# A transformer block on one core: fewer warm-up matmuls, two clamps on VectorE, a later wait in front of two transposes, and new queue orders

## The chip, the core and the metric

The kernel runs on one core of a Trainium2 chip. A core has five engines with a queue each: TensorE (PE) for matmuls and transposes, VectorE (DVE), ScalarE (ACT), GpSimd (POOL) and SyncE (SP), which issues most transfers. Every queue is worked off in order; a semaphore makes an instruction wait for one of another engine. Sixteen DMA engines move the data. The metric is the device time of one execution in microseconds, the median of several runs.

## The reference

One block of a transformer on 2048 tokens of width 448: normalization, linear attention with 16 heads of 28, a residual, normalization, a gated GELU layer of width 1792, a residual.

```python
phi = lambda t: jnp.where(t > 0, t + 1, jnp.exp(t)) + 1e-6
x  = A_x                                          # 1 x 2048 x 448
q, k, v = heads(_layernorm(x) @ A_wqkv)           # 16 heads of 28
pq, pk  = phi(q), phi(k)
kv  = einsum("bhsd,bhse->bhde", pk, v);  z = pk.sum(tokens)
o   = einsum("bhqd,bhde->bhqe", pq, kv) / (einsum("bhqd,bhd->bhq", pq, z) + 1e-6)
h   = x + o @ A_wo
n   = _layernorm(h)
out = h + (gelu(n @ B_w_gate) * (n @ B_w_up)) @ B_w_down
```

## The kernel before

The tokens are cut into 16 tiles of 128. Every piece of work on a tile is a named task on one engine. The kernel first builds all tasks with what they read and write, from which come the semaphores; the order of the tasks on each engine is written out by hand, name by name, in `ORDERS` (lines 14 to 62), one string each for PE, ACT, DVE, POOL and SP. A task cannot run before the one in front of it in its engine's string. A number in a name is a tile (for `q` tasks, a chunk of four tiles and a half; for `gu` tasks a running number).

The stages, and the names:

- **Start.** `warm1` and `warm0` (line 454) are matmuls of ones on PE that nobody reads; they keep PE busy until there is work. Their number is `WARM` (line 253), 38.
- **First normalization.** `bnst`, `bnag` on DVE gather mean and variance (lines 462, 463), `negm` on POOL negates the mean, `ln`, `rstd` on ACT make the reciprocal deviation, `norm` (line 486 on DVE for tiles 0 to 3, line 487 on POOL for the others) writes `xn`. Tiles 0 to 3 are transposed on PE (`tr`, line 495) and copied out on ACT (`ev`, line 523). For the others ACT copies 64 columns behind the tile (`dup`, line 525), and SP issues a DMA transpose (`xT`, line 526).
- **k and v.** `k` and `v` tasks of PE together compute both projections of a tile in two PSUM banks. A matmul uses 64 of 128 rows, so that two run side by side, one on the upper half (A), one on the lower (B); `k` has K on half A and V on half B, `v` the other way round. Where two tasks swap the halves of a bank, the second waits until the first is complete. `ek` (ACT) takes the exponential of K, `cl` (POOL, line 566) clamps it to 0 and 1, `ph` (DVE, line 568) makes pk of both, `evv` (ACT, line 570) copies V. `acc..a`, `acc..b` (PE) add pk and v into banks 6 and 7, with the halves swapped between a and b.
- **q.** `qa`, `qb` on PE, `eq` and `rq` (exponential, relu, lines 616, 617) on ACT, `cq` and `pq` on POOL and DVE.
- **Attention output.** `kz1`, `kz2` (DVE, lines 642, 643) make the masked kv, `nd` on PE multiplies it with pq, `rd`, `om` (DVE) divide. Tiles 0 and 1 are transposed on PE (`tro`), tiles 2 to 15 by a DMA transpose (`oT`, line 729). `wo` on PE applies the output matrix, `hr` (DVE, line 660) adds the residual.
- **Second normalization.** For tiles 0 and 1 `normh` and `wrap` on DVE write `hn` (`wrap`, line 695, copies its first 64 columns behind the tile), `trh` transposes seven blocks of it on PE (line 702; only the last block reads the wrapped columns), `evh` copies them out. The others go through POOL and a DMA transpose (`hT`, line 750).
- **The gated layer.** `gu` on PE, `ge` (Gelu, ACT, line 830), `hm` (product, DVE, line 832), `down` on PE, `out` (DVE, line 756), `dout` (SP). `tbl2` loads ACT's table for Gelu before the first `ge`.

SP's string also holds the loads: the tiles of x and the weights of q first, then `xT4` to `xT15`, then `dwo..` (4 loads) and `dwg0 dwu0 ... dwu6` (14 loads of 224 KB), then `oT2 oT3 dwd` (1568 KB) and the transposes of the gated stage. All are issued from SP in this order.

Tasks whose waits are given by position (`mw=True`) wait in front of the matmul that needs the buffer and not in front of the whole task; `emit` calls `W(n)` for that.

Of the kernel before, what the change touches and what calls it, by code (L numbers as in the profile page):

```python
# [7 lines left out]
ALU = mybir.AluOpType  # L8
# [4 lines left out]

ORDERS = (
# [47 lines left out]
)  # L62


# [145 lines left out]
def _c_mm(n, cnt=1):  # L210
    return cnt * (n / 2400.0 + 0.0025)
# [6 lines left out]
def _c_dve(n, rate=1.0):  # L218
    return 0.06 + n / 960.0 / rate
# [11 lines left out]
def bass_sequential_preLN__linear_attn_block__glu_gated_geglu__prompt_kernel(  # L231
    nc, A_x, A_wqkv, A_wo, B_x, B_w_gate, B_w_up, B_w_down, out, cfg=None
):
    cfg = dict(cfg or {})
    S, D, FF = 2048, 448, 1792
# [5 lines left out]
    EPS = 1e-6  # L241
# [4 lines left out]
    NQC = S // QCH  # L246
    N_PE_TR = 4
    STAT_GROUPS = [[0], [1], [2], [3]] + [[t, t + 1] for t in range(4, T, 2)]
    EV_DVE = cfg.get("ev_dve", ())
    N_DVE_NORM = cfg.get("n_dve_norm", 4)  # L250
    N_PE_A2 = 2
    B1_CHUNKS = [2, 2, 4, 4, 4]
    WARM = 38
    WARM2 = 8
    N_END = 4
    Q_LATE = cfg.get("q_late", 5)
# [2 lines left out]
    G = _Graph()  # L259
    es = ExitStack()  # L260
    with es:
# [14 lines left out]
        ident = sb("ident", [128, 128], BF16)  # L276
# [4 lines left out]
        mones = sb("mones", [GP, 4], F32)  # L281
        eps_t = sb("eps_t", [128, 1], F32)
        mhalf = sb("mhalf", [128, 2], F32)
# [5 lines left out]
        ln1 = sb("ln1", [128, T], F32)  # L289
# [3 lines left out]
        ln2 = sb("ln2", [128, T], F32)  # L293
        rs2 = sb("rs2", [128, T], F32)
        xn = sb("xn", [128, T, 512], BF16)
        e1 = sb("e1", [128, 3, D], BF16)
        tm1 = sb("tm1", [128, 3, D], BF16)
# [26 lines left out]
        b_ident, b_ones, b_mask2, b_mask3, b_mtmp, b_mones = (_Buf(n) for n in ("ident", "ones", "mask2", "mask3", "mtmp", "mones"))  # L324
# [5 lines left out]
        b_hn, b_hnd = bufs("hn", HN_R), bufs("hnd", HN_R)  # L330
        b_hnT = bufs("hnT", HR)
        b_e1, b_tm1, b_pk, b_v1 = bufs("e1", 3), bufs("tm1", 3), bufs("pk", 4), bufs("v1", 4)
# [10 lines left out]
        def bank(*b):  # L343
            return [b_ps[x] for x in b]
# [24 lines left out]
        def op(eng, fn, r, w, name, dur, key=None, after=()):  # L369
            if key is None:  # L370
                ik[0] += 0.01
                key = ik[0]
            return G.add(eng, fn, r=r, w=w, name=name, dur=dur, key=key, after=after)
# [129 lines left out]
        for ts in STAT_GROUPS:  # L503
# [6 lines left out]
            for t in ts:  # L510
                dve = t < N_DVE_NORM
# [12 lines left out]
                else:  # L524
                    op("act", lambda e, t=t: e.activation(xn[:, t, D:512], xn[:, t, 384:D], AF.Identity), [b_xn[t]], [b_xnd[t]], "dup%d" % t, 0.105, kln)
                    xt = G.add("sp", lambda e, tok=tok, t=t: e.dma_start_transpose(xnT[:, :, tok], xn[:, t, :]), r=[b_xn[t], b_xnd[t]], w=[b_xnT[t]],
                               name="xT%d" % t, kind="dmat", dur=1.25, key=t - 3.0, after=xts[-1:])
# [14 lines left out]
        def kv_tile(t):  # L542
            kk = 6.5 + 1.75 * t
# [4 lines left out]
            def kmm(s, o_, v, st_, sp_):  # L548
# [14 lines left out]
            i, ie = t % 4, t % 3  # L563
            psK3 = oK.rearrange("p (g e) -> p g e", g=NG)
            act_exp(lambda e: e.activation(e1[:, ie, :], oK, AF.Exp), bank(bk), [b_e1[ie]], "ek%d" % t, _c_act(D), kk)  # L565
            op("pool", lambda e: e.tensor_scalar(tm1[:, ie, :], e1[:, ie, :], 1.0 + EPS, 0.0, ALU.min, ALU.max),  # L566
               [b_e1[ie]], [b_tm1[ie]], "cl%d" % t, 0.53, kk)
            op("dve", lambda e: e.scalar_tensor_tensor(pk[:, i, :, 0:GW], psK3, EPS, tm1[:, ie, :].rearrange("p (g e) -> p g e", g=NG), ALU.max, ALU.add),  # L568
               bank(bk) + [b_tm1[ie]], [b_pk[i]], "ph%d" % t, _c_dve(D), kk)
            op("act", lambda e: e.activation(v1[:, i, :, 0:GW], oV.rearrange("p (g e) -> p g e", g=NG), AF.Identity),  # L570
# [92 lines left out]
        def a2_first(t):  # L663

            ka = -20.0 + 0.1 * t
            bnd, bh = FIRST_BK[t]
# [28 lines left out]
            op("dve", lambda e: e.tensor_copy(hn[:, sh, D:512], hn[:, sh, 0:64]), [b_hn[sh]], [b_hnd[sh]], "wrap%d" % t, 0.09, ka)  # L695
            tvh = psb[:, bh, 0:896].rearrange("p (k t) -> p k t", k=7)

            def ftrh(e):
                ins = None
                for k in (0, 1, 2, 4, 5, 6, 3):  # L700
                    ko = k * 128 if k < 4 else (k - 4) * 128 + 64
                    ins = e.transpose(tvh[:, k, :], hn[:, sh, ko:ko + 128], ident[:])
                return ins
            G.add("pe", ftrh, r=[b_hn[sh], b_hnd[sh], b_ident], w=bank(bh), name="trh%d" % t, dur=_c_mm(128, 7), key=ka)
            hv_ = hnT[:, :, (t % HR) * 128:(t % HR + 1) * 128]
            if t % 2 == 0:
                exp_tasks.append(op("act", lambda e: e.activation(hv_, tvh, AF.Identity), bank(bh), [b_hnT[t % HR]], "evh%d" % t, _c_act(896), ka))
# [205 lines left out]
```

## Time and profile before

| what | us |
|---|---|
| median of 3 runs | 196.21 (196.19 to 196.62) |
| the profiled execution | 196.7 |
| its span, first to last instruction | 194.9 |
| PE busy | 190.3 |
| DVE busy | 116.3 |
| ACT busy | 78.2 |
| POOL busy | 42.0 |

A row of the timeline reads: start and duration in us from the start of the span, engine, line, operation, output<-inputs, their shapes, number of instructions in a row; in brackets the idle time of the engine before it and what ended it. Neighbouring instructions of the same kind are merged, so that one row can hold several tasks. A `q` behind an engine's name marks its sequencer, which issues a transfer; a row `DMA to landing` tells how long the transfers of the row above took from issue to the end. PEld is the loading of weights into PE and overlaps PE. A busy PE is not PE at its peak: a matmul's row is some 0.2 us longer than the time after which the next one can start. A row of the windows has the stretch, its length, the granted clock, the share of the 16 DMA engines that is busy and the GB/s.

### The profile page before, as it was taken

Reading aid. Unit: us, or ns where it says so; the run is one execution under the profiler, and the core shown is the slowest. Engines: PE = TensorE matmul, PEld = TensorE weight load, DVE = VectorE, ACT = ScalarE, POOL = GpSimd, SP = SyncE. Lnnn points to the kernel's source line nnn. Section 1 sums busy time; section 2 is a strip of 40 time slices with the busy share of each in tenths; the row PEclk is TensorE's granted clock in tenths of the full one; section 3 lists DMA queues with packets and bytes.
Section 4 is the critical chain, followed back from the end, with each engine's and each line's share of the span. In section 5 each row is a group of like instructions: output and inputs, shape, how many; then the busy total and the mean of one; then the engine's idle time right before and its main releaser. Section 6 shows DMA issues by size and latency. Waiting matters only on the chain.

```text
span 194.9 us, 5336 instructions
## 1 busy us (share of the span) xinstructions
PE 190.3 (98%) x2192; PEld 137.9 (71%) x2192; DVE 116.3 (60%) x301; ACT 78.2 (40%) x205; POOL 42.0 (22%) x90
## 2 busy tenths in 40 slices
PE   7999999999999999999999999999999999999994
PEld 7556658754588977976675577877778779899554
DVE  2989735368998946843967745756735443431512
ACT  3689866669784212220442441233232442411100
POOL 3099974300050310500500500500500000000000
PEclk9999999999999999999999999999999999999999
DMA  6944558999836052152062250172040000010111
GB/s 191 377 116 97 81 110 185 247 248 205 260 103 110 15 101 50 50 105 62 10 129 46 46 106 2 30 117 51 5 94 28 23 0 0 3 47 3 47 47 47
DMA packets 37256, 17.53 MB, mean 90 GB/s; under 512 B 28272, under 2 KB 36336, under 8 KB 37232
## 3 DMA queue, kind: packets, MB, share of 16 engines
q1 hardware_dynamic: 36352, 16.45, 36.8%
q10 hardware_dynamic: 880, 0.75, 1.2%
q8 instruction: 17, 0.28, 0.6%
q14 instruction: 7, 0.06, 0.1%
HBM read 8.72 MB, written 1.84 MB: 54 GB/s over the span
## 4 chain that ended last, share of the span: by engine, by line
PE 96%; issue 1%; ACT 1%; DVE 1%; POOL 0%; DVEq 0%; ACTq 0%; POOLq 0%
PE ps L430 87%; PE ps L780 6%; PE ps L454 2%; DVE x_sb L660 1%; PE ps L495 1%; ACT xn L617 1%; PE ps L681 0%; ACT xnT L523 0%; PE ps L672 0%; DVE x_sb L756 0%; POOL ones_bf L395 0%; POOL eps_t L398 0%; ACT pqT L616 0%; DVEq L196 0%; ACTq L196 0%
## 5 line engine op out<-in xcount | busy, mean ns | idle before, releaser
L430 PE MATMUL ps<-hnT,wgu_sb 64*128 64x512 bf16 (+1 forms) x980 | 90.4, 333 | 0.0
L430 PEld LDWEIGHTS ps<-hnT,wgu_sb 64*128 64x128 bf16 x980 | 64.5, 94 | 18.6 <-DVE hh L832 1.7
L830 ACT ACTIVATE gl<-ps 128x256 bf16<-128x256 f32 x112 | 36.9, 381 | 89.3 <-PE ps L430 88.2
L832 DVE TENSOR_TENSOR hh<-ps,gl 128x256 bf16<-128x256 f32 x112 | 42.5, 415 | 35.7 <-ACT gl L830 31.5
L430 PE MATMUL ps<-wd_sb,hh 64*128 64x448 bf16 x336 | 34.4, 349 | 0.0
L430 PEld LDWEIGHTS ps<-wd_sb,hh 64*128 64x128 bf16 x336 | 25.6, 94 | 6.2 <-DVE x_sb L756 0.2
L430 PE MATMUL ps<-wkv_sb,xnT 64*128 64x448 bf16 x192 | 22.4, 350 | 0.4 <-ACT xnT L523 0.4
L462 DVE BATCH_NORM_STATS2 st<-x_sb 128x6 f32<-128x448 bf16 x32 | 18.7, 611 | 2.6 <-DMA x_sb<-in_A_x_dram 2.6
L756 DVE TENSOR_TENSOR x_sb<-ps,x_sb 128x448 bf16<-128x448 f32 (+1 forms) x17 | 9.9, 591 | 16.6 <-PE ps L430 9.8
L474 POOL TENSOR_SCALAR ln<-mv 128x2 f32<-128x2 f32 x7 | 1.6, 223 | 75.0 <-DVE mv L463 74.9
L568 DVE SCALAR_TENSOR_TENSOR pk<-ps,tm 128x448 bf16<-128x448 f32 x16 | 9.8, 620 | 9.6 <-POOL tm L566 7.1
L430 PE MATMUL ps<-xnT,wq_sb 64*128 64x512 bf16 x112 | 14.9, 377 | 0.2 <-ACT xn L617 0.2
L430 PEld LDWEIGHTS ps<-wkv_sb,xnT 64*128 64x128 bf16 x192 | 10.1, 94 | 6.3 <-issue 0.8
L430 PE MATMUL ps<-wo_sb,oT 64*128 64x448 bf16 x98 | 12.1, 350 | 0.1
L660 DVE TENSOR_TENSOR x_sb<-ps,x_sb 128x448 bf16<-128x448 f32 x16 | 9.4, 618 | 4.6 <-PE ps L430 4.4
L780 PE MATMUL ps<-wd_sb,hh 128*128 128x448 bf16 (+1 forms) x70 | 10.8, 315 | 0.0
L566 POOL TENSOR_SCALAR tm<-e 128x448 bf16<-128x448 bf16 x16 | 8.9, 559 | 6.4 <-ACT e L565 5.5
L487 POOL TENSOR_SCALAR hn<-x_sb,nm,rs 128x448 bf16<-128x448 bf16 x14 | 10.0, 720 | 0.8 <-POOL rs L476 0.2
L565 ACT ACTIVATE e<-ps 128x448 bf16<-128x448 f32 x16 | 8.5, 541 | 3.5 <-PE ps L430 2.2
L780 PEld LDWEIGHTS ps<-wd_sb,hh 128*128 128x128 bf16 x70 | 6.7, 98 | 4.3 <-issue 0.4
L655 DVE TENSOR_TENSOR o_sb<-ps,rd 128x448 bf16<-128x448 f32 x16 | 9.4, 612 | 0.1
L570 ACT ACTIVATE v<-ps 128x448 bf16<-128x448 f32 x16 | 8.4, 542 | 2.1 <-PE ps L430 2.1
(69 smaller groups left out, 140.4 us busy)
## 6 DMA issues: line engine op xcount, KB each, us to landing
out_dram<-x_sb SPq DMA_DIRECT2D x15, 112.0 KB, 1.7
wgu_sb<-in_B_w_gate_dram SPq DMA_DIRECT2D x7, 224.0 KB, 6.1
wgu_sb<-in_B_w_up_dram SPq DMA_DIRECT2D x7, 224.0 KB, 6.4
wd_sb<-in_B_w_down_dram SPq DMA_DIRECT2D x1, 1568.0 KB, 8.3
x_sb<-in_A_x_dram SPq DMA_DIRECT2D x2, 448.0 KB, 5.3
wkv_sb<-in_A_wqkv_dram ACTq DMA_DIRECT2D x2, 336.0 KB, 3.7
x_sb<-in_A_x_dram SPq DMA_DIRECT2D x3, 224.0 KB, 4.2
wo_sb<-in_A_wo_dram SPq DMA_DIRECT2D x2, 336.0 KB, 4.4
```

Source lines behind the costliest of these rows:

```text
L430: ins = e.matmul(o_, l_, r_, start=s_, stop=p_, **kw)
L462: op("dve", lambda e: e.bn_stats(st[:, t, :], src_ap), [b_src], [b_st[t]], "%sbnst%d" % ("" if mv is mv1 else "h", t), 0.53, key, after=after)
L487: return lambda e: e.tensor_scalar(dst, src[:, t, :], nm[:, t:t + 1], rs[:, t:t + 1], ALU.add, ALU.mult)
L565: act_exp(lambda e: e.activation(e1[:, ie, :], oK, AF.Exp), bank(bk), [b_e1[ie]], "ek%d" % t, _c_act(D), kk)
L566: op("pool", lambda e: e.tensor_scalar(tm1[:, ie, :], e1[:, ie, :], 1.0 + EPS, 0.0, ALU.min, ALU.max), [b_e1[ie]], [b_tm1[ie]], "cl%d" % t ...
L568: op("dve", lambda e: e.scalar_tensor_tensor(pk[:, i, :, 0:GW], psK3, EPS, tm1[:, ie, :].rearrange("p (g e) -> p g e", g=NG), ALU.max, ALU ...
L655: op("dve", lambda e: e.tensor_tensor(o_sb[:, so, oc:oc + D].rearrange("p (a e) -> p a e", e=28), nd3[:, :, 0:28], rd[:, i, :].unsqueeze(2 ...
L660: op("dve", lambda e: e.tensor_tensor(h_sb[:, u, :], ps[:, b, 0:D], x_sb[:, u, :], ALU.add), bank(b) + [b_x[u]], [b_h[u]], "hr%d" % u, 0.5 ...
L756: op("dve", lambda e: e.tensor_tensor(x_sb[:, t, c0:c1], ps[:, bk, c0:c1], h_sb[:, t, c0:c1], ALU.add), bank(bk) + [b_h[t]], [bo], "out%d% ...
L780: ins = e.matmul(ps[:, bk, c0:c1], hh[:, j, hsl(t)], wd_sb[:, j, c0:c1], start=(j == 0), stop=(j == NJ - 1))
L830: G.add("act", lambda e, gi=gi, cs_=cs_, psG=psG: e.activation(gl[:, gi, cs_], psG[:, cs_], AF.Gelu_apprx_tanh), r=bank(BK_G[i]), w=[b_glh ...
L832: op("dve", lambda e, dst=dst, srcU=srcU, srcL=srcL: e.tensor_tensor(dst, srcU, srcL, ALU.mult), bank(BK_U[i]) + [b_glh], [b_ar[j_][t % HR ...
```

## The change

Three edits in the code, and new strings for all five engines.

- `WARM` is 33 instead of 38.
- `cl14` and `cl15`, the clamps of exp(K), run on DVE instead of POOL.
- `trh0` and `trh1` wait for `normh` in front of their first block, and for `wrap` in front of the last one.

```diff
+    CL_DVE = cfg.get("cl_dve", (14, 15))
...
-    WARM = 38
+    WARM = 33
...
-            op("pool", lambda e: e.tensor_scalar(tm1[:, ie, :], e1[:, ie, :], 1.0 + EPS, 0.0, ALU.min, ALU.max),
-               [b_e1[ie]], [b_tm1[ie]], "cl%d" % t, 0.53, kk)
+            op("dve" if t in CL_DVE else "pool", lambda e: e.tensor_scalar(tm1[:, ie, :], e1[:, ie, :], 1.0 + EPS, 0.0, ALU.min, ALU.max),
+               [b_e1[ie]], [b_tm1[ie]], "cl%d" % t, _c_dve(D, 4.0) if t in CL_DVE else 0.53, kk)
...
-            def ftrh(e):
+            def ftrh(e, W):
                 ins = None
-                for k in (0, 1, 2, 4, 5, 6, 3):
+                for n, k in enumerate((0, 1, 2, 4, 5, 6, 3)):
+                    if n in (0, 6):
+                        W(n)
...
-            G.add("pe", ftrh, r=[b_hn[sh], b_hnd[sh], b_ident], w=bank(bh), name="trh%d" % t, dur=_c_mm(128, 7), key=ka)
+            G.add("pe", ftrh, r=[b_hn[sh], (b_hnd[sh], 6), b_ident], w=bank(bh), name="trh%d" % t, dur=_c_mm(128, 7), key=ka, mw=True, pdt=_c_mm(128))
```

The strings differ in many places. Those that matter below, before and after, engine by engine:

```
PE   v5 k6 qa01 v6 qb01 k7 acc3a acc4a v7
     v5 acc3a k6 qa01 v6 qb01 acc4a k7
PE   k11 k12 v11 v12 k13 acc8b acc9b v13 k14 acc9a k15 acc10a v14
     k11 acc8b k12 acc9b v11 v12 k13 acc9a acc10a v13 k14 k15 v14
PE   acc12a acc12b acc13b qa20 acc13a acc14a qb20 acc14b acc15b acc15a qa11
     acc12a acc12b acc13b acc13a acc14a qa20 acc14b acc15b qb20 acc15a qa11
PE   qa31 wo2a qb31 wo2b trh1 trh0 nd4a nd4b gu1
     qa31 wo2a wo2b trh1 trh0 qb31 nd4a nd4b gu1
ACT  ek7 evv7 evv8 dup14 ek8 dup15 evv9 ek9 ek10 evv10
     ek7 evv7 dup12 ek8 evv8 ek9 dup14 evv9 dup15 ek10 evv10
ACT  hln0 hrstd0 eq14 evh0 tbl2 ge1_0 ge1_1 rq14
     hln0 hrstd0 evh0 eq14 tbl2 ge1_0 ge1_1 ge0_1 ge0_0 ge3_1 ge3_0 rq14
DVE  bnst6 ph0 bnst7
     bnst6 bnst7 ph0
DVE  ph13 ph14 ph15 kz1 kz2
     ph13 cl14 ph14 cl15 ph15 kz2 kz1
POOL negm8 cl2 cl3 norm8 norm9 cq1 cq0 negm10 negm12 cl4 norm10 norm11 cl5 norm13 norm12 cl6
     negm8 cl2 norm9 cl3 norm8 negm12 cq1 cq0 negm10 cl4 norm13 cl5 norm10 negm14 norm11 cl6
POOL cl6 negm14 cq3 cq2 cl7 norm14
     cl6 opad2 cq3 cq2 cl7 norm12 norm14
```

On SP the order up to `dwu6 oT2 oT3 dwd` is the same; later some neighbours of the same kind change places (`oT4 oT5`, `dout0 dout1` and the like). In the gated stage `gu` tasks stand closer together before a `down` task (`gu49 gu48 gu51 gu50 down8a` where `gu49 gu48 down8a gu50 gu51` stood), and pairs of `ge` and `hm` tasks change places.

More of the change, by code (lines that the diff above doesn't have):

```diff
@@ L15 @@
     "warm1 warm0 tr0 tr1 k0 v0 k1 tr2 tr3 v1 k2 acc0a k3 v2 v3 qa00 acc0b acc1b qb00 k4 acc1a acc2a v4 k5 acc2b acc3b"
[4 rows of a table removed]
[4 rows of a table added]
     " wo6b down0b nd8a gu11 nd8b gu10 gu13 gu12 down2a wo8a down2b wo8b gu15 nd10a gu14 nd10b gu17 gu16 gu19 gu18 gu21"
     " wo10a wo10b gu20 nd12a gu23 nd12b gu22 gu25 gu24 gu27 gu26 wo12a down4a wo12b gu29 nd14a gu28 nd14b gu31 down4b"
[36 rows of a table removed]
[31 rows of a table added]
+    "ones eps mhalf mones powwarm ident mask_a opad mask_b mask_c negm4 cl0 norm4 norm5 negm6 cl1 norm6 norm7 negm8"
[4 rows of a table added]
     "dx0 dx1 dx2 dwv_t dx4 dx6 dx8 dx12 dwq dwq_t dwq_u pqones xT4 xT5 xT6 xT7 xT8 xT9 xT10 xT11 xT12 xT13 xT14 xT15"
[3 rows of a table removed]
[3 rows of a table added]
 )
```

83 rows, old and new, of the table ORDERS are left out of this document.

## The prediction

> **What bounds the kernel now.** I read the page first, then the chain of waits, then the timeline around each place that the change touches.
>
> ```profile
> span 194.9 us, 5336 instructions
> PE 190.3 (98%) x2192; PEld 137.9 (71%) x2192; DVE 116.3 (60%) x301; ACT 78.2 (40%) x205; POOL 42.0 (22%) x90
> PE 96%; issue 1%; ACT 1%; DVE 1%; POOL 0%; DVEq 0%; ACTq 0%; POOLq 0%
> ...
> 2.00 4.17 PE ps L454 x38
> 37.55 0.05 issue
> 40.26 0.05 issue
> 52.26 1.17 DVE x_sb L660 x2
> 62.84 40.46 PE ps L430 x552
> 103.35 78.37 PE ps L430 x776
> ```
>
> The chain is TensorE nearly throughout. From 62.84 to 181.72 us two pieces of matmuls follow each other with 0.05 us between them: nothing can be won there without removing matmuls, and the change removes none. What can move lies before 63 us: the start, and the places where TensorE waits. So the question is how much earlier TensorE starts, and whether what it needs later also comes earlier. The profiled execution took 196.7 us: 194.9 us of span and 1.8 us around it. It is 0.49 us above the median of the runs, 196.21 us.
>
> **The change, part by part.**
>
> *Fewer warm-up matmuls.* The start, in order of time:
>
> ```profile
> 5.21 0.37 DVE L486 TENSOR_SCALAR xn<-x_sb,mv,rs 128x448 bf16<-128x448 bf16 x1
> 5.97 0.40 DVE L486 TENSOR_SCALAR xn<-x_sb,mv,rs 128x448 bf16<-128x448 bf16 x1
> 6.10 0.96 PE L495 MATMUL ps<-ident,xn 64*128 64x64 bf16 x20
> 6.68 1.08 ACT L523 ACTIVATE xnT<-ps 128x512 bf16<-128x512 bf16 x2 [0.83 <-PE ps L495]
> 7.43 0.74 PE L430 MATMUL ps<-wkv_sb,xnT 64*128 64x448 bf16 x6 [0.36 <-ACT xnT L523]
> 9.76 0.75 PE L495 MATMUL ps<-ident,xn 64*128 64x64 bf16 x20
> ```
>
> The 38 warm-ups of line 454 take 4.17 us, 0.11 each; five fewer free TensorE 0.55 us earlier, at 5.55. But tr0 needs norm0, which ends at 5.58. With a hand-over of 0.06 us (an estimate; DVE's last residual add, below, ends at 53.42 and its matmul starts at 53.47) tr0 starts at 5.64 instead of 6.10. Its copy ev0 and then k0 follow at their present distances, so k0 starts at 6.97: **-0.46 us**. The rest of the 0.55 is lost to norm0. tr1 needs norm1 (ends 6.37) and moves by only 0.14, but k1 is not due for another 1.5 us.
>
> The 20 transposes of tr0 and tr1 take 0.96 us, the same 20 of tr2 and tr3 0.75: the clock doubled in between. [...]
>
> *The reordered POOL queue gives a little back.* The order of norm8, norm9 and the clamps changes:
>
> ```profile
> 16.75 1.19 POOL L626 TENSOR_SCALAR tm<-e 112x512 bf16<-112x512 bf16 x2
> 17.39 1.29 DVE L627 SCALAR_TENSOR_TENSOR pqT<-ps,tm 112x512 bf16<-112x512 f32 x2
> 18.74 0.30 PEld L430 LDWEIGHTS ps<-wkv_sb,xnT 64*128 64x128 bf16 x6 [0.29 <-DVE pqT L627]
> ```
>
> Today k6 waits for pq0 (ends 18.68), which waits for the q clamps cq1, cq0 on POOL. POOL is full here and moves earlier with its first input. In the new order negm12 comes ahead of cq1, one operation of 0.2 us, so pq0 moves by only 0.25. But acc3a (0.10) is put before k6 and fills part of it. **+0.11 us**, bounds 0 and 0.25. TensorE is then 0.35 earlier.
>
> *The clamps of tiles 14 and 15 on VectorE.*
>
> ```profile
> 37.96 0.62 DVE L568 SCALAR_TENSOR_TENSOR pk<-ps,tm 128x448 bf16<-128x448 f32 x1 [1.71 <-POOL tm L566]
> L749 DVE COPY hn<-hn x14: 264/268/333, 58.6 to 141.1; 128x448 bf16<-128x448 bf16 x14
> ```
>
> The trace has no such clamp on DVE. Nearest rows: a copy of 128x448 (0.27 us) below, the normalization of 128x448 (0.37) above; I take 0.27, since a clamp has constants as the copy has none and norm0 reads two scalars per row. It hides in the 1.71 us in which DVE waits for POOL; if that cover were gone it would cost 0.27 to 0.37 each. ph14 and ph15 come some 0.4 and 0.8 us earlier, and acc13a, acc14a move ahead of qa20. That moves the bank swaps, it doesn't remove them: before, two sit back to back (the issue pieces at 37.55 and 40.26); after, acc12a-acc12b and acc13b-acc13a do. **0**, bounds -0.12 and +0.12.
>
> *The transposes of xn wait for ACT.* This is the part the diff hides. ACT runs its queue in order, and the new order is "ek9 dup14 evv9 dup15" where it was "dup14 ek8 dup15 evv9 ek9".
>
> ```profile
> 25.59 0.25 ACT L525 ACTIVATE xn<-xn 128x64 bf16<-128x64 bf16 x1
> 26.25 0.26 ACT L525 ACTIVATE xn<-xn 128x64 bf16<-128x64 bf16 x1
> 27.23 0.55 ACT L570 ACTIVATE v<-ps 128x448 bf16<-128x448 f32 x1 [0.72 <-PE ps L430]
> 27.67 0.98 ACT L565 ACTIVATE e<-ps 128x448 bf16<-128x448 f32 x2
> ...
> L526 SPq DMA_TRANSPOSE xnT<-xn x2: 1216/1216/1217, 26.1 to 27.4; - x2
> 28.64 3.19 SPq L364 DMA_DIRECT2D wo_sb<-in_A_wo_dram  x4
> 45.48 2.51 SPq L729 DMA_TRANSPOSE oT<-o_sb  x2
> ```
>
> dup14 and dup15 (the rows of line 525) stand before the wait for v9 now, which ends at 27.23. Afterwards dup14 stands behind ek9, which needs v9: ek9 starts at 27.23 - 0.35 = 26.88, dup14 0.44 later (the distance of evv9 and ek9) and ends at 27.57. So xT14 is issued at 27.6 instead of 26.1, xT15 1.3 later, and dwo, the first of 18 weight loads behind them on SP, at about 30.2 instead of 28.64: **1.6 us later** (a second path, norm12 put behind cl7 on POOL, gives 1.8; if dup14 moved as TensorE does, 1.2). The weights themselves have cover: the last lands at 48.4 (below), gu1 starts at 54.13. But these loads fill the DMA engines, and behind them come oT2 and oT3:
>
> ```profile
> 44.00:46.00 2.00, 1.00 1.02 242
> L364 SPq DMA_DIRECT2D wgu_sb<-in_B_w_up_dram x1: 597/597/597, 40.9 to 40.9; - x1
> DMA to landing us min/median/max: 7.5/7.5/7.5
> ...
> DMA to landing us min/median/max: 2.6/3.1/3.5
> oT<-o_sb SPq DMA_TRANSPOSE x14, 2.5
> pqT<-ones_bf SPq DMA_DIRECT2D x1, 16.0 KB, 5.3
> ```
>
> The DMA share at 44 to 46 us is 1.02 (242 GB/s): the stream is bound by bandwidth, so it ends as much later as it starts later. Its last load lands at 40.9 + 7.5 = 48.4; oT2, which at its median would land at 48.0, lands at 45.48 + 3.5 = 49.0, and oT3 at 46.7 + 2.6 = 49.3. A load of 16 KB took 5.3 us behind the first weights. So what is issued behind a full queue lands behind it. Shifted by 1.6, oT2 lands at 50.6 and oT3 at 50.9.
>
> [...]
>
> ```profile
> 50.07 0.94 PE L430 MATMUL ps<-wo_sb,oT 64*128 64x448 bf16 x8
> 50.83 0.83 PE L430 MATMUL ps<-xnT,wq_sb 64*128 64x512 bf16 x6
> 53.04 0.22 PE L430 MATMUL ps<-kvz,pqT 64*128 64x116 bf16 x1
> 53.47 0.82 PE L430 MATMUL ps<-kvz,pqT 49*128 49x116 bf16 x15 [0.21 <-DVE x_sb L660]
> 54.13 0.60 PE L430 MATMUL ps<-hnT,wgu_sb 64*128 64x256 bf16 x8
> ...
> 61.77 1.81 PE L430 MATMUL ps<-wo_sb,oT 64*128 64x448 bf16 x14
> 63.42 0.82 PE L430 MATMUL ps<-hnT,wgu_sb 64*128 64x256 bf16 x12
> ```
>
> wo2a is due at 50.07 - 0.35 = 49.72 and can start at about 50.65 (0.93 lost). Its second matmul needs oT3, at 50.95, which adds about 0.2. **+1.15 us**; bounds 0.6 (1.2 later) and 1.5 (1.8 later). Behind wo2a TensorE's queue holds everything; nothing fills the hole.
>
> *After it.* wo2a and wo2b now stand back to back, as wo4a and wo4b do: those take 61.77 to 63.42, 1.65 us, where wo2a takes 50.83 - 50.07 = 0.76 for eight matmuls and six need 0.57. The swap of halves costs 0.32 there. In return qb31 stands before nd4a and covers the two residual adds that it waits for, 53.04 to 53.47, 0.43. **-0.10 us**, bounds -0.4 and +0.3. trh's split wait buys nothing: its copies are done while wo2a waits. eq14 now stands directly before the table load, so the first Gelu can come some 0.2 us late, of which a started pair of matmuls takes up most; **+0.05**, bounds 0 and 0.2. The other reorderings (gu, hm, out) lie under the unbroken matmuls after 62.84: 0, bounds -0.1 and +0.2.
>
> Sum: -0.46 + 0.11 + 0 + 1.15 - 0.10 + 0.05 = +0.75: 197.45 us by the profiled execution. The median lies 0.49 below it. If that is a shorter start, the new kernel doesn't gain it, since its start is set by norm0; if it is the profiling, it carries over whole (196.96). I take the middle, **197.2 us**; own range 196.8 to 197.7.
>
> **The rivals.**
>
> *A, the transposes are not held up (not slower).* The stream starts late but ends early enough, or oT2 and oT3 pass it. It decides at wo2a: its slack now is 50.07 - 49.3 = 0.8 us, so up to 0.4 us of lateness costs nothing after a gain of 0.35. For it: the weights' issues run 7.5 us ahead of their landings. Against it: a share of 1.02. Price: -0.46 + 0.11 - 0.10 + 0.05 = -0.40; 196.3 us by the profiled execution, 195.8 by the median.
>
> [...]
>
> *C, the front isn't shortened* because the median execution already starts early: 196.21 + 0.05 + 1.15 - 0.10 + 0.05 = 197.4, inside the forecast's range.
>
> **How the numbers follow.** Forecast with C: 0.62; A: 0.28; B: 0.10. The range from 195.8 (A) to 197.8 leaves out B and A's tail. A measurement of this kernel tells 0.3%, 0.59 us, from no change, so faster means below 195.62, slower above 196.80. A with its terms at their good ends falls below in half its cases: faster 0.14. The other half of A and 0.05 of the forecast's low end are the same: 0.19. Slower: 0.67.
>
> **What would show it.** tr0 at 5.6 and k0 at 7.0 show the first term; dwo issued after 30 us on SP and oT3 landing near 51 show the stream; an idle TensorE of about 1 us before wo2a's matmuls, ended by DMA, shows the loss; no wait for DVE before nd4a shows the small gain. I am wrong if dwo is issued before 29.2, or if oT3 lands before 50; k0's matmuls at the slow pace would show B.

## The result and the profile after

The changed kernel takes 197.58 us in the median of 8 runs (197.07 to 200.83), the kernel before 196.31 (196.17 to 196.74) in 8 runs on the same chip: a ratio of 1.0055, interval 1.0041 to 1.007. The change costs about one microsecond. The run of 200.83 us, at a clock of 0.991, is left out of the ratio. The profiled execution of the changed kernel is its fastest, 197.07 us; that of before, 196.7 us, was one of its slower ones. So the two profiles differ by 0.4 us of span where the medians differ by 1.27 (1.04 between the medians once that run is left out).

The page of the changed kernel, first the span, then the shares of the chain of waits:

```profile
span 195.3 us, 5326 instructions
...
PE 90%; DVE 4%; ACT 2%; DMA 2%; issue 1%; SPq 0%; DVEq 0%
```

PE's share of the chain is 90% where it was 96%. Some 12 us more of the chain (6% of the span) lie outside TensorE, and where they do is the first thing to read. Some 4.5 of them lie ahead of k0, where the chain now runs through the first normalization and not through the warm-ups, and cost nothing. TensorE's timeline at the places that the prediction named:

```profile
5.65 0.41 PE L496 MATMUL ps<-ident,xn 64*128 64x64 bf16 x10 [0.46 <-DVE xn L487]
6.86 0.74 PE L431 MATMUL ps<-wkv_sb,xnT 64*128 64x448 bf16 x6
...
18.38 0.74 PE L431 MATMUL ps<-wkv_sb,xnT 64*128 64x448 bf16 x6
...
48.48 1.04 PE L431 MATMUL ps<-xnT,wq_sb 64*128 64x512 bf16 x8 [0.19 <-ACT xn L618]
49.65 2.19 PE L431 MATMUL ps<-wo_sb,oT 64*128 64x448 bf16 x14
...
53.32 0.81 PE L431 MATMUL ps<-kvz,pqT 64*128 64x116 bf16 x16
53.97 8.29 PE L431 MATMUL ps<-hnT,wgu_sb 64*128 64x256 bf16 x140
...
63.65 0.60 PE L431 MATMUL ps<-hnT,wgu_sb 64*128 64x256 bf16 x8
```

These rows are tr0, k0, k6, qa31, wo2a with wo2b, nd4a with nd4b, gu1 and gu4. One row of before has not been shown yet, qa31:

```profile
49.21 1.04 PE L430 MATMUL ps<-xnT,wq_sb 64*128 64x512 bf16 x8 [0.19 <-ACT xn L617]
```

Cut at these tasks, the two spans add up as follows (each number is the difference of two start times above and in the prediction):

| stretch | before | after | difference | predicted |
|---|---|---|---|---|
| start to k0 | 7.43 | 6.86 | -0.57 | -0.46 |
| k0 to k6 | 11.31 | 11.52 | +0.21 | +0.11 |
| k6 to qa31 | 30.47 | 30.10 | -0.37 | 0 |
| qa31 to gu1 | 4.92 | 5.49 | +0.57 | +1.15 and -0.10 |
| gu1 to gu4 | 9.29 | 9.68 | +0.39 | +0.05 |
| gu4 to the end | 131.48 | 131.65 | +0.17 | 0 |
| sum | 194.9 | 195.3 | +0.40 | +0.75 |

The first row flatters the change, because the two executions differ in the clock. The trace records the step of TensorE's clock from half to full at 6.86 us in the execution of before and at 4.57 us in this one, and the warm-ups start 0.107 us apart ahead of it and 0.056 behind it.

The loss lies in two places that follow each other, the wait before wo2a and the first matmuls of the gated layer. For the first, SP's timeline (xT12 to xT15, dwo and its three companions, oT2 and oT3) and the landing times of the last two:

```profile
25.30 6.09 SPq L527 DMA_TRANSPOSE xnT<-xn  x4
31.44 2.39 SPq L365 DMA_DIRECT2D wo_sb<-in_A_wo_dram  x4
...
44.75 2.51 SPq L732 DMA_TRANSPOSE oT<-o_sb  x2
...
DMA to landing us min/median/max: 4.0/4.4/4.8
```

dwo is issued at 31.44, 2.8 us later than before (28.64). oT2 lands at 44.75 + 4.8 = 49.55, and wo2a starts at 49.65; oT3 lands at 46.0 + 4.0 = 50.0, and the rest of wo2a starts at 50.13, as the chain below shows. Before, oT3 had landed at 49.4 and nothing waited. The predicted landing was 50.9: the stream started later than foreseen, but in this execution it also ran faster. The windows (stretch, length, busy time of PE, PEld, DVE, ACT and POOL, granted clock, DMA share, GB/s):

```profile
44.00:46.00 2.00, 2.00 (x22) 0.83 (x18) 1.97 (x6) 1.83 (x4) 0.00 (x0) 1.00 1.04 298
```

It moved 298 GB/s where the execution of before moved 242 in the same window, at the same full share. For the second place, the chain of waits (start, length, what):

```profile
49.87 0.19 DVE mv L464
...
50.13 0.93 PE ps L431 x7
...
52.77 0.92 ACT hnT L710
53.68 0.91 ACT pqT L617
54.62 1.28 ACT L853
55.91 0.39 ACT gl L833
56.40 0.75 DVE hh L835 x2
57.15 0.53 DVE pqT L619 x2
...
57.74 0.74 DVE hh L835 x2
...
58.70 0.74 DVE pqT L620
...
59.84 0.68 DVE hh L835 x2
60.56 2.47 PE ps L431 x35
```

From 52.77 to 60.56 TensorE doesn't set the end: ScalarE does (evh0, eq14, the table load tbl2, ge1), then VectorE (hm1, cq14 and cq10, hm0, wrap3, pq10, wrap2, hm3), and gu5 starts when hm3 frees its bank. Before, the chain was matmuls from 53.47 us on. VectorE's timeline of before at hm0, pq12 and hm3:

```profile
57.88 0.75 DVE L832 TENSOR_TENSOR hh<-ps,gl 128x256 bf16<-128x256 f32 x2 [0.24 <-ACT gl L830]
...
58.92 0.68 DVE L619 TENSOR_TENSOR pqT<-xn,pqT 112x1024 bf16<-112x1024 bf16 x1
59.52 0.75 DVE L832 TENSOR_TENSOR hh<-ps,gl 128x256 bf16<-128x256 f32 x2
```

Measured from the start of gu1, hm0 starts at 3.75 us before and at 3.77 after, so cq14 and cq10, which stand ahead of it now, cost nothing. hm3 starts at 5.39 before and at 5.79 after (59.76 on VectorE), the whole 0.4: between the two stands pq10, which takes 1.04 us (58.62 to 59.66), where pq12 with 0.68 stood.

The first line of the chain wants care: it names VectorE ahead of wo2a, but wo2a reads only oT and wo_sb. The releaser shown is the last of several by time; the landing of oT3 at 50.0 is what wo2a needed.

### The profile page after: what moved, and what is told of

It reads as the page before. It is cut to its first block, busy times and chain, and to the rows that moved or that the text cites. A ratio compares the mean times of both kernels' runs of the same rounds, so it can differ in the third digit from the quotient of the medians.

```text
span 195.3 us, 5326 instructions
## 1 busy us (share of the span) xinstructions
PE 189.9 (97%) x2187; PEld 126.9 (65%) x2187; DVE 117.2 (60%) x303; ACT 77.9 (40%) x205; POOL 41.9 (21%) x88
## 4 chain that ended last, share of the span: by engine, by line
PE 90%; DVE 4%; ACT 2%; DMA 2%; issue 1%; SPq 0%; DVEq 0%
PE ps L431 82%; PE ps L783 6%; DMA x_sb<-in_A_x_dram 2%; DVE hh L835 1%; DVE st L463 1%; ACT L853 1%; DVE x_sb L661 1%; PE ps L496 1%; ACT hnT L710 0%; ACT pqT L617 0%; PE ps L705 0%; DVE pqT L620 0%; PE ps L689 0%; PE ps L682 0%; PE ps L673 0%
## 5 line engine op out<-in xcount | busy, mean ns | idle before, releaser
L431 PE MATMUL ps<-hnT,wgu_sb 64*128 64x512 bf16 (+1 forms) x980 | 91.8, 333 | 0.1
L431 PEld LDWEIGHTS ps<-hnT,wgu_sb 64*128 64x128 bf16 x980 | 61.2, 94 | 23.9 <-DVE hh L835 5.2
L431 PE MATMUL ps<-wd_sb,hh 64*128 64x448 bf16 x336 | 35.3, 349 | 0.0
L431 PEld LDWEIGHTS ps<-wd_sb,hh 64*128 64x128 bf16 x336 | 21.1, 94 | 10.9 <-DVE x_sb L759 0.2
L431 PE MATMUL ps<-wo_sb,oT 64*128 64x448 bf16 x98 | 13.0, 350 | 0.4
L482 POOL TENSOR_SCALAR nm<-mv 128x2 f32<-128x2 f32 x13 | 3.0, 227 | 39.5 <-DVE mv L464 39.1
L488 POOL TENSOR_SCALAR hn<-x_sb,nm,rs 128x448 bf16<-128x448 bf16 x14 | 10.7, 768 | 0.8 <-POOL rs L477 0.2
L431 PEld LDWEIGHTS ps<-wo_sb,oT 64*128 64x128 bf16 x98 | 6.3, 94 | 4.5 <-PE ps L431 1.5
```

Source lines behind the costliest of these rows:

```text
L431: ins = e.matmul(o_, l_, r_, start=s_, stop=p_, **kw)
L482: op("pool", lambda e: e.tensor_scalar(nm[:, a:b], mv[:, a:b, 0], -1.0, None, ALU.mult), b_mv[a:b], b_nm[a:b], "%snegm%d" % ("" if mv is m ...
L488: return lambda e: e.tensor_scalar(dst, src[:, t, :], nm[:, t:t + 1], rs[:, t:t + 1], ALU.add, ALU.mult)
```

## The experiments

The kernel before was run beside each group: 196.5 us median in 32 runs beside the first four experiments, 196.66 in 25 beside the next four, 196.4 in 23 beside e9 to e11, 196.32 in 9 beside e12. Ratios are to before's runs of the same group; medians of different groups compare less well, since before's own differ by 0.35. Orders are given as the part of the string that differs.

### e1 and e2: the copies for the transposes early again, in the changed kernel

```diff
 ACT
-ek8 evv8 ek9 dup14 evv9 dup15 ek10 evv10
+ek8 evv8 dup14 ek9 dup15 evv9 ek10 evv10
```

> The changed kernel with two names moved in ACT's order: dup14 ahead of ek9, dup15 ahead of evv9. Theory (late weight stream): xT15 is issued near 29.1 us instead of 30.2 and dwo near 30.4 instead of 31.4; about 1.0 us less of wo2a's wait for oT2 and oT3 remains, so 0.5 to 1.0 us faster than the changed kernel, near 196.8 us. Rival (the loss is in the new order behind wo2a: back-to-back halves, and VectorE and GpSimd in the first gated tiles): no change from 197.6 us.

Measured: 198.02 us median (196.85 to 200.13, 9 runs), ratio 1.0067, interval 1.0036 to 1.0099. A miss, and a useful one. SP's and TensorE's timelines of e1, with the landing times of oT2 and oT3:

```profile
31.04 2.40 SPq L365 DMA_DIRECT2D wo_sb<-in_A_wo_dram  x4
...
DMA to landing us min/median/max: 5.0/5.4/5.8
...
50.58 0.35 PE L431 MATMUL ps<-wo_sb,oT 64*128 64x448 bf16 x1 [1.09 <-DVE hn L487]
51.09 1.72 PE L431 MATMUL ps<-wo_sb,oT 64*128 64x448 bf16 x13 [0.16 <-DVE hn L487]
```

dwo came only 0.4 us earlier, and not even this is the copies': xT12 to xT14 are issued at the same times as in the changed kernel, to 0.01 us, and only the issues of xT14 and xT15 took less, 3.0 us together instead of 3.4. Something ahead of dup14 held the queue: xT12, whose copy dup12 now waits for norm12 behind cl7. And in this execution the transposes took 5.0 to 5.8 us to land instead of 4.0 to 4.8: oT3 landed at 46.0 + 5.0 = 51.0, and wo2a's two parts started at 50.58 and 51.09 where the changed kernel's started at 49.65 and 50.13. So the loss at this place is some 0.9 us larger here, though dwo was issued earlier: the stream moved 251 GB/s from 44 to 46 us and not 298. e2 adds the other half:

```diff
 POOL, on top of e1
-cl4 norm13 cl5 ... cq2 cl7 norm12
+cl4 norm12 cl5 ... cq2 cl7 norm13
 ACT
-dup13 dup10 ln14 ... evv7 dup12 ek8
+dup12 dup10 ln14 ... evv7 dup13 ek8
```

> As e1, and norm12 and norm13 (POOL), dup12 and dup13 (ACT) change places, so that the transposes are ready in the order in which SP issues them. Theory: dwo near 29.2 us, no wait for a transfer at wo2a, 196.1 to 196.5 us, the whole loss undone. Rival: 197.4 to 197.6 us.

Measured: 196.8 us median (196.42 to 198.71, 12 runs), ratio 1.0028, interval 1.0007 to 1.0049. dwo is issued at 30.08 instead of 31.44 (29.2 was expected), and the median is 0.8 us lower. It lies between its theory and its rival, 0.3 us above before: oT2 landed at 49.78, and wo2a, which was due at 49.3, started at 49.87. There are two paths to a late dwo, one through dup14 and dup15, one through norm12 and dup12; undoing the first alone gains little while the second holds. 1.4 us of the delay stay: xT13, whose copy now stands where xT12's stood, is issued 0.6 us later than before, and the issue of xT15 takes 2.14 us instead of 1.22.

### e3: the late copies alone, in the kernel before

```diff
 ACT
-evv8 dup14 ek8 dup15 evv9 ek9 ek10 evv10
+evv8 ek8 evv9 ek9 dup14 dup15 ek10 evv10
```

> The kernel before with dup14 and dup15 moved behind ek9 in ACT's order, nothing else. Theory: dwo near 30.6 us instead of 28.6, oT3 lands near 51, wo2a waits about 1 us for transfers: 197.0 to 197.5 us. Rival: the kernel before has none of the other reorderings, so it stays at 196.3 us.

Measured: 197.36 us median (196.61 to 197.87, 12 runs), ratio 1.0042, interval 1.0029 to 1.0056. SP's and TensorE's timelines of e3, with the landing times of oT2 and oT3:

```profile
30.63 2.50 SPq L364 DMA_DIRECT2D wo_sb<-in_A_wo_dram  x4
...
DMA to landing us min/median/max: 4.4/4.7/5.1
...
50.15 0.35 PE L430 MATMUL ps<-wo_sb,oT 64*128 64x448 bf16 x1 [0.43 <-DVE st L462]
50.70 0.91 PE L430 MATMUL ps<-wo_sb,oT 64*128 64x448 bf16 x7 [0.21 <-DMA oT<-o_sb]
```

Two copies of 0.26 us on ScalarE, moved behind two and three other instructions, cost 0.86 us in the median 22 us later. Nothing else in this kernel differs from before. The second row names its releaser rightly, the transpose, which lands at 46.2 + 4.4 = 50.6.

### e5 and e6: the loads of wo moved ahead of the transposes

```diff
 SP, in the changed kernel; dwo no longer waits for a transpose
-xT9 xT10 xT11 xT12 xT13 xT14 xT15 dwo dwo_t dwo_u dwo_s dwg0
+xT9 dwo xT10 dwo_t xT11 dwo_u dwo_s xT12 xT13 xT14 xT15 dwg0
```

> The changed kernel with the four loads of wo issued in SP's idle time between xT9 and xT12, so that the 14 gate and up weights follow xT15 directly. Theory (late weight stream): the first of those 14 is issued near 31.4 us instead of 33.9, the last lands near 47 us, oT3 lands near 48.6, wo2a doesn't wait for a transfer: 1.0 to 1.5 us faster than the changed kernel, 196.0 to 196.5 us. Rival (the loss lies in the order on TensorE and VectorE behind wo2a): 197.4 us as before.

Measured: 197.41 us median (196.5 to 199.13, 12 runs), ratio 1.006, interval 1.0035 to 1.0085: no gain that can be told, and the 1.0 to 1.5 us of the theory not at all. The wait at wo2a is gone, but another has come, so that the rival's time came out without the rival's reason. TensorE's timeline of e5 at k12:

```profile
31.04 0.74 PE L431 MATMUL ps<-wkv_sb,xnT 64*128 64x448 bf16 x6 [0.96 <-DMA xnT<-xn]
```

xT12 now stands behind two weight loads, is issued at 25.77 and lands at 30.90, too late for k12; in the changed kernel it took 2.4 us to land. That the loads alone hold it is not shown: the changed kernel's xT13, with no load just ahead of it, is issued at 26.54 and lands at 30.76. In e6 pq10 on VectorE was moved as well, from ahead of wrap2 to behind pq14:

> As e5, and pq10 moves behind pq14 in VectorE's order. In the changed kernel gu5 lost 0.29 us behind hm3, which stood behind a pq10 that took 1.04 us beside GpSimd's normh2. Theory: this loss goes too, 0.2 to 0.3 us faster than e5, and faster than the kernel before (195.7 to 196.2 us). Rival (pq10 costs the same wherever it stands): as e5.

Measured: 197.42 us median (196.88 to 198.13, 8 runs), ratio 1.0042, interval 1.0027 to 1.0058. The median is that of e5, so the 0.2 to 0.3 us that were expected did not come.

### e10 and e11: the changed kernel with the old order up to the end of the k/v stage

```diff
 PE up to acc12a, ACT up to evv15, DVE up to ph13, POOL up to cl13
-the changed strings
+the strings of before
```

> The changed kernel with the orders of before on all four engines up to the end of the k/v stage (PE up to acc12a, ACT up to evv15, DVE up to ph13, POOL up to cl13); 33 warm-ups, both clamps on VectorE, the split wait of trh and all later orders stay changed. Theory (the late dup14, dup15 and norm12 hold up xT14, xT15, then dwo, then oT2 and oT3): dwo is issued by 28.3, oT3 lands by 49.4, wo2a loses under 0.25 us, and the median is 196.3 to 196.8, since the loss at gu3 and gu5 (0.3 to 0.4) stays. Rival (the loss comes from the later orders, that is the tail of the attention stage and the gated stage): 197.2 to 197.6, as the changed kernel.

Measured: 196.56 us median (196.47 to 198.37, 12 runs), ratio 1.0033, interval 1.0012 to 1.0055. The median is 1.0 us below the changed kernel's and within 0.2 of before's; the later orders, the clamps and the 33 warm-ups are still the changed ones. The order of the k/v stage (with the copies and normalizations for the transposes in it) carries most of the loss. The profiled execution of e10, at 198.15 us, shows something else. Its TensorE timeline at k0 and v0:

```profile
6.98 1.30 PE L431 MATMUL ps<-wkv_sb,xnT 64*128 64x448 bf16 x6
...
8.71 2.12 PE L431 MATMUL ps<-wkv_sb,xnT 64*128 64x448 bf16 x12
```

The six matmuls of k0 take 1.30 us where they take 0.74 in the changed kernel's profile, and the pace doubles only some way into k1. The trace records the step to the full clock at 10.40 us, some 3.5 us later than in the execution of before (6.86). It is what was to show rival B, k0's matmuls at the slow pace, in one execution. (The clock column of the windows reads 1.00 ahead of this first step in every execution, and is of no use there.) e11 has the same strings and pq10 behind pq14:

```diff
 DVE
-wrap3 pq10 wrap2 hm3_1 hm3_0 pq12 pq14 hm2_1
+wrap3 wrap2 hm3_1 hm3_0 pq12 pq14 pq10 hm2_1
```

> The kernel of the run above, and pq10 on VectorE behind pq14 instead of ahead of wrap2. Theory (pq10 beside GpSimd's normh2 makes hm3_0 late, and gu5 waits for it): gu5 loses under 0.1 us and the median is 0.2 to 0.3 below the run above, 196.0 to 196.5. Rival (the wait only moves to a later gu): no difference from the run above.

Measured: 196.69 us median (196.51 to 198.38, 9 runs), ratio 1.0041, interval 1.0014 to 1.0069. SP's and TensorE's timelines of e11:

```profile
28.27 3.45 SPq L365 DMA_DIRECT2D wo_sb<-in_A_wo_dram  x4
...
49.66 1.74 PE L431 MATMUL ps<-wo_sb,oT 64*128 64x448 bf16 x14
```

dwo is back at 28.27 and wo2a with wo2b takes 1.74 us instead of 2.19, with no wait. Moving pq10 gained nothing in the median, as in e6. In the profile of e11 gu1 to gu4 takes 9.41 us instead of the changed kernel's 9.68, but gu4 to gu20 takes 40.84 instead of 40.56: gu12 waits 0.25 us longer instead. That is the rival's case: the wait only moved.

### e4, e7 and e8: the warm-ups and the clamps, each alone in the kernel before

```diff
-    WARM = 38
+    WARM = 33        (e4)
+    WARM = 20        (e7)
```

> The kernel before with 33 warm-up matmuls. Theory: tr0 starts at 5.64 us, bound by norm0; 0.1 to 0.45 us faster than before, 195.9 to 196.2 us, more where the clock is released late. Rival (the front is worth nothing, since the clock or a later wait takes it back): 196.3 us.

Measured: 196.24 us median (196.07 to 197.88, 12 runs), ratio 0.9996, interval 0.998 to 1.0012: no difference that the ratio can tell, but it holds one execution of 197.88. The other eleven lie between 196.07 and 196.46, while 16 of the 32 of before beside them lie above 196.5, and the median is 0.26 us lower. Its profiled execution starts k0 at 6.83, as the changed kernel does. Why no more than this is won is in e8's start, a kernel with 38 warm-ups. TensorE's timeline of e8 at the last warm-ups and tr0:

```profile
4.83 0.28 PE L454 MATMUL ps<-ones_bf 128*128 128x128 bf16 x2
5.79 0.41 PE L495 MATMUL ps<-ident,xn 64*128 64x64 bf16 x10 [0.69 <-DVE xn L486]
```

In this execution the clock was up at 3.81 us, the 38 warm-ups were over at 5.1 us, and tr0 waited 0.69 us for norm0. Fewer warm-ups can win nothing there. They can in an execution like the profiled one of before, where the clock was up at 6.86 us only and the 38 warm-ups lasted to 6.17, with norm0 done at 5.58.

> The kernel before with 20 warm-up matmuls: TensorE idles from 4.2 to 5.6 us. [...]

Measured: 197.74 us median (197.69 to 198.33, 5 runs), ratio 1.0067, interval 1.0054 to 1.0079. Windows of e7, columns as above:

```profile
4.00:8.00 4.00, 2.01 (x31) 0.88 (x28) 3.21 (x9) 2.42 (x7) 0.00 (x0) 0.99 1.10 367
8.00:11.00 3.00, 2.98 (x24) 1.37 (x24) 2.60 (x9) 2.02 (x8) 1.05 (x3) 0.50 1.07 354
11.00:14.00 3.00, 3.00 (x44) 1.71 (x46) 2.51 (x8) 2.51 (x8) 2.41 (x5) 0.94 0.12 25
```

What was tried here is whether it costs anything that TensorE idles before tr0; how long the loss would be was the author's estimate, from a term that no run shows. All five executions lost over 1 us. In the profiled one the clock was up (from 4.53 us), then fell to half from just before 8 us to about 11.4 (a mean of 0.94 over 3 us is 0.36 us at half), some 3.4 us. Ahead of the fall TensorE had had little to do, 2.01 us of 4, with no pause over 1.6 us; that this is the reason is inferred, and how little work is too little is not shown. The full clock first comes at a different time in each of these profiles: 3.81 us in e8, 4.53 here, 4.57 in the changed kernel, 6.86 in before, 10.40 in e10. What sets it no run shows.

With 33 warm-ups such a loss comes in some executions only. Of the 90 executions of the nine kernels here that have 33 (the changed one, e1, e2, e4, e5, e6, e9, e10, e11), 17 took over 1.5 us more than the fastest of the same kernel; of the 124 with 38 (before, e3, e8, e12) none did. Two kernels that differ in nothing else are e4 with 1 of 12 and before with 0 of 97. That the clock is behind it is recorded for the one of the 17 that has a profile, e10's; three more show the mean clock of 0.991 that e7's executions have (0.990 to 0.991); for the others it is inferred from their times.

e8 moved the two clamps alone:

```diff
 DVE
-ph13 ph14 ph15 kz1
+ph13 cl14 ph14 cl15 ph15 kz1
```

> The kernel before with the clamps of tiles 14 and 15 on VectorE, nothing else. Theory: each takes near 0.27 us in VectorE's idle time, acc14 and acc15 don't wait for them today, so within 0.12 us of the kernel before, 196.3 us. Rival (VectorE is late there for kz1): 0.3 to 0.6 us slower.

Measured: 196.56 us median (196.33 to 197.1, 10 runs), ratio 1.0002, interval 0.9992 to 1.0011. The two clamps on VectorE in e8 (fastest, median and slowest in ns, first and last start in us); on GpSimd one takes 562 ns:

```profile
L566 DVE TENSOR_SCALAR tm<-e x2: 277/277/277, 36.8 to 38.1; 128x448 bf16<-128x448 bf16 x2
```

### e9 and e12: the order behind wo2a, and parts put together

```diff
 e9: the kernel before with WARM = 33
 PE
-qa31 wo2a qb31 wo2b trh1 trh0 nd4a
+qa31 wo2a wo2b trh1 trh0 qb31 nd4a
 ACT
-eq14 evh0 tbl2
+evh0 eq14 tbl2
```

> The kernel before with 33 warm-ups and the changed order behind wo2a: wo2a wo2b trh1 trh0 qb31 nd4a on TensorE, evh0 ahead of eq14 on ScalarE. Theory (the -0.10 term: back to back halves cost 0.32, qb31 covers 0.43 of the wait of nd4a): nd4a loses 0.2 to 0.25 instead of 0.66, wo2b starts 0.3 late, and the median is 196.1 to 196.3. Rival (the split halves cost more than the cover gives): 196.4 to 196.8.

Measured: 196.89 us median (196.78 to 198.46, 8 runs), ratio 1.0044, interval 1.0021 to 1.0068: a little above the rival's range, and by another mechanism than the rival's. In its profile the swap does win what was forecast: k0 to gu1 takes 46.58 us where e4 needs 46.72. The loss comes behind gu1: gu1 to gu4 takes 10.04 us instead of 9.29. e12 was to join this order with the changed orders of TensorE's k/v stage and the clamps, at 38 warm-ups, and with rq14 moved out of the first Gelus:

> The kernel before, 38 warm-ups, its ScalarE, VectorE and GpSimd orders up to the attention stage (so dup14, dup15 and norm12 where they were), with four parts of the change alone: TensorE's order of the acc, k and q tasks, the order wo2a wo2b trh1 trh0 qb31 nd4a, evh0 ahead of eq14 with rq14 behind ge3_0, and both clamps on VectorE. Theory (these parts win 0.2 to 0.4 between k6 and qa31 and 0.1 to 0.2 behind wo2a, lose about 0.1 at gu3 and gu5, and neither the stream nor the clock is touched): dwo at 28.0 to 28.7, wo2a loses under 0.25, median 195.9 to 196.3 where before shows 196.3 to 196.7, and no execution more than 1.4 above the fastest. Rival (gu3 and gu5 lose 0.4 or more, as in the changed kernel): 196.4 to 196.8.

Measured: 197.28 us median (197.06 to 197.52, 5 runs), ratio 1.0045, interval 1.0031 to 1.0058: slower than its theory and its rival. VectorE's timeline of e12, and gu3's first weights on PEld:

```profile
54.80 0.43 DVE L618 TENSOR_SCALAR pqT<-pqT 112x1024 bf16<-112x1024 bf16 x1 [0.93 <-ACT pqT L616]
...
57.92 2.95 PEld L430 LDWEIGHTS ps<-hnT,wgu_sb 64*128 64x128 bf16 x56 [0.74 <-DVE hh L832]
```

cq14 needs eq14, which is now behind evh0, and through qb31 behind trh0. It stands first in VectorE's queue here, so that 0.93 us of VectorE pass empty just before the stretch in which it is the bound; all that is behind cq14, hm1 too, comes late, and gu3 waits 0.74 us for hm1. e9 has the same two numbers. The changed kernel spares itself this: its DVE string has cq14 and cq10 behind hm1. Nor did TensorE's new k/v order win anything by itself in e12: k6 to qa31 takes 30.52 us, with the old ScalarE order beneath it, against 30.47 in before. No version tried here beats the kernel before by more than its measurement tells.

## Why the prediction held, point by point

**The sum.** 197.2 was forecast, 197.58 measured, slower as forecast, and by the mechanism that was given the largest term. But several terms were off and cancelled in part, as the table shows.

**The front, -0.46.** The times fit (tr0 at 5.65 for a forecast of 5.64, bound by norm0, k0 at 6.86 for 6.97), but that is luck in part: with the clock up at 4.57 us, as here, 38 warm-ups would have ended at about 5.5 (an estimate: five more at the 0.056 us between the last ones), before norm0, so that leaving out five of them won nothing in this execution. As a gain of the kernel the term was too large: e4's median is 0.26 us lower, and its ratio cannot be told from 1. Rival C was right in the executions whose clock is up early, at 3.81 us in e8's profile and at 4.57 here.

**The POOL order, +0.11.** +0.21, within its bounds of 0 and 0.25.

**The clamps, 0.** Right: e8's ratio is 1.0002, and the clamp took 0.277 us there for an estimate of 0.27.

**The bank swaps and acc tasks, 0.** k6 to qa31 got 0.37 us shorter, outside the bounds of 0.12. e12 has TensorE's new order without this gain (30.52 us), so it needs one of the other new orders of the stage, of ScalarE, VectorE or GpSimd; e11 has the old ones and no gain (30.46). It was not split further.

**The stream, dwo 1.6 us late.** The mechanism was right: e3 and e10 show it from both sides, and in all fourteen profiles oT2 lands 0.47 to 0.55 us behind the last of the weight loads. The sizes were wrong, in both directions. ScalarE's part came as forecast; ScalarE's timeline of the changed kernel, dup12 and dup14:

```profile
25.02 0.26 ACT L526 ACTIVATE xn<-xn 128x64 bf16<-128x64 bf16 x1 [0.94 <-POOL xn L488]
...
27.28 0.25 ACT L526 ACTIVATE xn<-xn 128x64 bf16<-128x64 bf16 x1
```

dup14 ends at 27.53 for a forecast of 27.57. But it held nothing up here, since SP was busy with the issue of xT13 until 27.80. The step that failed is the choice between the two paths: the one through norm12 stood in a bracket, and it is the one that bound. Its size was right, for xT12 is issued at 25.30 instead of 23.47, 1.83 us late against 1.8. A further 0.97 had no term: the issue of xT14 took 2.19 us where it took 1.22 before. So dwo came 2.8 us late, beyond the upper bound.

Then the step "it ends as much later as it starts later" failed too. The last load landed at 49.02 instead of 48.45, 0.57 us late, because the stream ran at up to 298 GB/s, and oT3 landed at 50.0 and not at 50.9. In e1, e2 and e3, where dwo was 2.4, 1.4 and 2.0 us late, the last load was 1.5, 0.9 and 1.1 late. That the two errors nearly cancel is luck. The prediction called itself wrong if oT3 landed before 50; in the trace it is 49.99, so by the letter it was, while the mechanism held. For wo2a's term of +1.15, e11, which has the same order and no wait, needs 4.73 us from qa31 to gu1 and the changed kernel 5.49: it measured 0.76 in the fastest execution. e1's timeline gives 0.9 more at the same place, which is how the median can lie 0.5 above the profiled time; the rate in the other runs of the changed kernel was not recorded.

**After it, -0.10.** Right: nd4a no longer waits for DVE, e9 gives -0.14 against e4, and e11 -0.19 against before (4.73 for 4.92).

**The first Gelu, +0.05.** This is the term that was mis-sized most in proportion. That the first Gelu would come 0.2 us late was right (55.91 - 53.97 = 1.94 us behind gu1, against 55.87 - 54.13 = 1.74). That "a started pair of matmuls takes up most" was not, and gu1 to gu4 lost 0.39. Of this 0.27 is pq10: e11, which has it behind pq14, takes 9.41 us. The other 0.12 is left at gu3, which waits 0.19 us for hm1 in both. The step looked at one instruction's lateness and not at VectorE's new order behind it, in which a pq10 of 1.04 us stands ahead of hm3.

**The other reorderings, 0.** gu4 to the end took 0.17 more, within the bound of 0.2.

**Rival A** (not held up) fell, but narrowly: wo2a was due at 49.34, and oT2 and oT3 landed at 49.56 and 49.99. **Rival B**, a clock that comes up later with 33 warm-ups than with 38, was taken for a shift of all executions, at 0.10 and a price of 1.2 us. No run shows the term from which that price was worked out. In its place e10's profile shows the step at 10.40 us where before's has it at 6.86, and in e9 to e11 eight of 29 executions take 1.6 to 1.9 us more than the fastest; for the seven of them without a profile it is inferred from the times that the clock is behind it.

## What to carry to other kernels

When an order is changed, follow the longest queue behind each moved instruction to the last thing it issues: in e3 a 0.26 us copy delayed a transpose, that the weight loads, those two later transposes, and TensorE 22 us on. Before moving work from behind one stage into the next, ask which engine is tight in the next one; a wait covered on TensorE was paid back on VectorE. Warm-up work that is spare in one execution (in e8's profile TensorE waited 0.69 us behind it) may not be in another (with 20 warm-ups all five executions of e7 lost over 1 us, with 33 17 of 90 took over 1.5 us more than the fastest), so judge it by the spread of many runs and not by the median alone.

## What the runs showed of the hardware that was not expected

The same VectorE multiplication runs at two speeds. pq in the changed kernel (five of them), then in e11:

```profile
L620 DVE TENSOR_TENSOR pqT<-xn,pqT x5: 675/679/1039, 42.6 to 61.0; 112x1024 bf16<-112x1024 bf16 x5
```

```profile
L620 DVE TENSOR_TENSOR pqT<-xn,pqT x5: 681/682/686, 42.9 to 60.9; 112x1024 bf16<-112x1024 bf16 x5
```

The slow one is pq10 at 58.62 us, while GpSimd runs normh3 and normh2. In e1, e2, e5 and e10, which have pq10 at the same place, it takes 1.04 us too; in e6 and e11, where it stands over 2 us later, 0.68. GpSimd's two instructions are slow as well at that place. GpSimd's timeline of the changed kernel, then of before:

```profile
57.08 2.04 POOL L488 TENSOR_SCALAR hn<-x_sb,nm,rs 128x448 bf16<-128x448 bf16 x2
```

```profile
57.11 1.41 POOL L487 TENSOR_SCALAR hn<-x_sb,nm,rs 128x448 bf16<-128x448 bf16 x2
```

They stay slow in e11 without pq10 beside them (2.01 us), so that for GpSimd's part another neighbour must count. The traces point to cq14 and cq10: in the seven profiles in which these start with normh3 (the changed kernel, e1, e2, e5, e6, e10, e11) normh3 takes 1.20 to 1.25 us, and in the seven others 0.71 or 0.72. No run moved them alone.

The issue of a transpose on SP, usually 1.2 us, took 2.19 us for xT14, and xT13 landed 4.2 us after its issue. In the traces of before, the changed kernel, e1 and e5 a load of 16 KB of instructions starts at 28.2 to 29.0 us, and single packets of the transposes take 0.9 to 1.8 us just behind it where 0.02 is usual; whether the one causes the other was not tried. And the rate of one and the same stream of weights, at a full DMA share (1.01 to 1.04), lay between 240 and 298 GB/s in the window from 44 to 46 us of before, the changed kernel and e1 to e3; what sets it stayed open.
